# A memory update's tile copied out of PSUM whole, and a new table by slot

## The chip, the cores and the metric

The kernel runs on one core of a Trainium2 chip. The time is device time of that core in microseconds (us). The kernel before took 998.64 us, the median of three runs (998.44 to 998.71). An engine is named as the profile names it: PE is TensorE's matmuls and PEld its weight loads, DVE is VectorE, ACT ScalarE, POOL GpSimd, and SP the engine that issues the DMAs.

## The reference, cut to what matters

Two attention blocks A and B with a compressive memory read the same input x (2048 x 640) and are mixed by a gate per token. Each block has 32 heads of 20 channels and goes over four segments of 512 tokens:

```python
for s in range(N):
    qs, ks, vs = q[:, :, s], k[:, :, s], v[:, :, s]
    logits = jnp.einsum("bhqd,bhkd->bhqk", qs, ks) * scale + mask
    p = _softmax(logits, axis=-1)
    a_dot = jnp.einsum("bhqk,bhkd->bhqd", p, vs)
    pq = phi(qs)
    num = jnp.einsum("bhld,bhde->bhle", pq, M)
    den = jnp.einsum("bhld,bhd->bhl", pq, z)[..., None] + 1e-6
    a_mem = num / den
    o = g * a_mem + (1.0 - g) * a_dot
    outs.append(o)
    pk = phi(ks)
    M = M + jnp.einsum("bhld,bhle->bhde", pk, vs)
    z = z + jnp.einsum("bhld->bhd", pk)
```

phi(t) is t + 1 above zero and exp(t) below; the mask is causal. M (20 x 20 a head) and z (20 a head) are the memory; the last two lines are its update, which the change is about.

## The kernel before, in words

**Tiling.** The 640 channels are five tiles m of 128. A pair of block and segment is a t from 0 to 7 (block t % 2, segment t // 2). For each t there are jobs of TensorE: the projections q and k by tile, v by half, and the output projection o. Each product is split into high and low parts and into the two halves of the array, 64 rows each, so that two matmuls can run side by side. Eight quads of four heads in each t give 64 units i. A unit has scores for the row maxima (`s_unit`, L1288, read by VectorE at L1275), scores transposed for the exponentials (`t_unit`, L1372, read by ScalarE at L1364, masked by POOL at L1365), and the product with v (`pv_unit`, L1392). All of these take one of the eight PSUM banks and give it back when the reading engine is through.

**The memory's update.** M and z of a block lie in five tiles `mbd` of 128 partitions by (heads of the tile) x 21 columns: 7 heads and 147 columns, or 8 and 168 for m = 2. Only where a row's channel belongs to the column's head is the entry wanted. After a `pv_unit`, `updates()` takes up to three tiles whose keys are there and lets TensorE make them in one bank, side by side (L1031). For each tile it goes over four windows of 32 partitions, and each window makes only the two or three heads that touch its rows, 42 or 63 columns. What stands in the tile's other columns of the bank is left from whatever used the bank before. `updated()` then has VectorE copy the four windows out (`take`, L1052), into `mbd` itself in the first segment, and into one of two tiles `mt` in the later ones. POOL sets to zero what is not an own head, by two selections (`keep_own_heads`, L377 and L381), and in the later segments adds the tile to `mbd` (L1057). `mt` is free again after the add; the bank when the copies of all its updates are through. Because the copies fill only the windows, `mbd` and `mt` are set to zero once at the start (L373).

**What sets the order.** Nothing is scheduled by hand on the chip: a planner in the kernel plays the run through with costs for each piece, and emits each engine's instructions in the order in which its play reaches them. `put(engine, cost, emit, then, prio)` queues a piece on ScalarE (A), VectorE (D), POOL (G) or the DMA queue (S); where two engines could do it, the one with less queued work gets it. TensorE's pieces are emitted one by one, each half of the array with its own clock (`op`), and a bank is taken when the play holds it free. The engines run their queues in order, so where a piece is later on the chip than in the play, everything behind it on its engine waits, and so does TensorE when the bank that it takes next is not yet empty. In the play an update costs TensorE 8 x `UPD` = 8 x (63 / 1200 + 0.0027) = 0.4416 us, its copies begin 0.2 us after its own matmuls and cost VectorE 0.44 us, and POOL's part costs 0.8 or 1.34 us. A table `RULES` gives 66 slots, one for each unit and two more, an order of the unit's ten pieces and seven numbers that shift when they are due (span, calm, lag, room, hold, wait, wait2).

Of the kernel before, what the change touches and what calls it, by code (L numbers as in the profile page):

```python
# [19 lines left out]
D = 640  # L20
# [12 lines left out]
LO = [P * m // DH for m in range(KT)]  # L33
# [9 lines left out]
def tile_gated_mix_infini_attn(  # L43
# [17 lines left out]
    nc = tc.nc  # L61
# [26 lines left out]


    RULES = {  # L90
# [66 lines left out]
    }  # L157
    rule = {}
    DONE = {"A": 0.27, "D": 0.26, "G": 0.22, "S": 0.0}
# [13 lines left out]
    def first_of(dur):  # L173
        return dur[0] if isinstance(dur, tuple) else dur

    def start_next(e):
        if busy[e] or not ready[e]:
            return
        if e == "S":
            begin_at = max(dma_free[0] - BACKLOG, lands[-LANES] if len(lands) >= LANES else 0.0)  # L180
            if begin_at > clk[0]:
                if not held[0]:
                    held[0] = True
                    at(begin_at, resume)
                return
        _, _, dur, emit, then = heapq.heappop(ready[e])
        base = first_of(dur)
        if base is not dur:
            dur = dur[1] if busy["G"] else dur[0]
        busy[e] = True  # L190
        emit()

        def end():
            busy[e] = False
            load[e] -= base
            if then and e == "S":
                then()
            elif then:
                at(clk[0] + DONE[e], then)
            start_next(e)  # L200

        at(clk[0] + dur, end)
# [9 lines left out]
    def put(e, dur, emit, then=None, prio=5):  # L212
        heapq.heappush(ready[e], (prio, next(seq), dur, emit, then))
        load[e] += first_of(dur)
        start_next(e)
# [115 lines left out]
    mbds = [[const.tile([P, HI[m] - LO[m] + 1, E1], F32, name=f"mbd{b}_{m}") for m in range(KT)] for b in range(2)]  # L331
# [34 lines left out]
    def ones_tiles():  # L366
        for t in vst:
            h = t[:, :, :H * E1].rearrange("p n (h e) -> p n h e", e=E1)
            nc.gpsimd.memset(h[:, :, :, DH], 1.0)
            nc.gpsimd.memset(h[:, :, H // 2, :12], 1.0)  # L370
            nc.gpsimd.memset(t[:, :, H * E1:], 1.0)
        for t in (*mbds[0], *mbds[1], *mt_store.free):
            nc.gpsimd.memset(t, 0.0)  # L373

    def keep_own_heads(t, m):
        nh, off = HI[m] - LO[m] + 1, P * m - DH * LO[m]
# [113 lines left out]
    for t in range(8):  # L490
        a = 0 if t == 0 else 8 * t - EARLY
# [511 lines left out]
    mt_store = Store([sb.tile([P, 8, E1], F32, tag=f"mt{i}", name=f"mt{i}", bufs=1) for i in range(2)])  # L1003
# [1 line left out]

    upd_due = deque()
    upd_run = set()
    UPD = 63 / 1200.0 + 0.0027

    def windows(m):  # L1010
        for j in range(4):
            f0 = P * m + 32 * j
            a, c = f0 // DH, (f0 + 31) // DH + 1
            yield slice(32 * j, 32 * j + 32), a, c

    def updates():
# [6 lines left out]
        for x in todo:  # L1023
# [5 lines left out]
            for n in range(NB):  # L1029
                for r, a, c in windows(m):  # L1030
# [4 lines left out]
                    )  # L1035
            now[0] += 8 * UPD
            upd_run.add((t, m))
# [3 lines left out]
    def updated(t, m, pkn, v, done):  # L1041
        s = t // 2
        mbd = mbds[t % 2][m]
        nh = HI[m] - LO[m] + 1

        def end():
            upd_done.add((t, m))

        def take(dst):
            for r, a, c in windows(m):  # L1050
                h = slice(a - LO[m], c - LO[m])
                nc.vector.tensor_copy(dst[r, h, :], v[r, h, :])  # L1052

        def got(tmp):
            def add():
                keep_own_heads(tmp[:, :nh, :], m)
                nc.gpsimd.tensor_tensor(out=mbd, in0=mbd, in1=tmp[:, :nh, :], op=ALU.add)  # L1057

            put("D", 0.44, lambda: take(tmp), lambda: (
                done(), put("G", 1.34, add, lambda: (mt_store.give(tmp), end()), prio=2)), prio=3)  # L1060

        big.give(pkn)
        if s == 0:
            put("D", 0.44, lambda: take(mbd), lambda: (
                done(), put("G", 0.8, lambda: keep_own_heads(mbd, m), end, prio=2)), prio=3)
        else:
            mt_store.want(1, got)
# [695 lines left out]

    warm_up()
    put("G", 6.0, small_tiles, prio=0)
    put("G", 2.8, ones_tiles, prio=1)
    big.want((F32,) * 4, lambda *rows: (x_first_rows.extend(rows), x_first.give(*rows[:3])))
    for k in range(KT):
        if k < len(HEAD0):
# [9 lines left out]
    for i in range(66):  # L1779
# [11 lines left out]
        for j in range(10):  # L1791
            fill_to(marks[i] - rule["hold"] + rule["span"] * (j + 1) / 10 * (marks[i + 1] - marks[i]))
            c = todo[0]
            if c == "S" and i + LEAD < 64 and "T" in todo and not S(i + LEAD, 0)() and T(i, 0)():
                c = "T"
# [63 lines left out]
```

## Time and profile before

| | before |
|---|---|
| median of three runs | 998.64 us (998.44 to 998.71) |
| the profiled execution's own time | 997.83 us |
| its span, first to last instruction | 996.1 us |
| granted clock of TensorE | 1.000 |
| copies of line 1052 | 120 |
| groups of updates on TensorE | 12, six of two tiles and six of three |

The profile is of one execution. The span is cut into what each engine did; "busy" on PE is modelled, so the waits of PE and PEld say more than its share. In a row of a group stand line, engine, operation, output and input with shapes, count, then busy us and mean ns of one, then the idle time in front of them and what ended it. In a row of the timeline stand start and length in us, the instruction, its count, and in brackets the idle time before it and who ended it.

### The profile page before, as it was taken

How to read it: one execution, taken by the hardware profiler on the slowest of the kernel's cores; microseconds unless marked ns; L12 is line 12 of the kernel's file. 1: busy time of each engine (PE TensorE's matmuls, PEld its weight loads, DVE VectorE, ACT ScalarE, POOL GpSimd, SP SyncE). 2: the span in 40 equal slices, each digit the busy share in tenths (PEclk: the TensorE clock that was granted, in tenths of full speed). 3: DMA queues.
4: the chain of work that ended last, by engine and by line, in shares of the span. 5: the costliest groups of instructions: out<-in, count | busy, mean ns of one | idle time of the engine just before them, and what ended most of it. 6: DMA issues, size and time to landing. Idle time of an engine off the chain costs nothing.

```text
span 996.1 us, 31535 instructions
## 1 busy us (share of the span) xinstructions
PE 979.4 (98%) x11559; PEld 821.2 (82%) x11559; DVE 814.0 (82%) x2904; ACT 654.4 (66%) x1310; POOL 604.5 (61%) x1052
## 2 busy tenths in 40 slices
PE   9999999999999999999999999999999999999998
PEld 7987888778897888987888877889788987879776
DVE  4796978887798977897879988888788997799874
ACT  5366777676586667685685746776577575675572
POOL 5455656766466765675654676576656664666561
PEclk9999999999999999999999999999999999999999
DMA  7987889898797876976759796789667987887521
GB/s 248 311 281 237 291 234 299 261 279 262 239 307 238 272 214 202 319 241 187 225 173 311 212 283 199 211 270 269 195 214 226 295 279 217 239 251 209 142 90 65
DMA packets 146453, 236.47 MB, mean 237 GB/s; under 512 B 12949, under 2 KB 45882, under 8 KB 145978
## 3 DMA queue, kind: packets, MB, share of 16 engines
q1 hardware_dynamic: 146298, 234.46, 76.4%
q8 instruction: 91, 1.49, 0.6%
q14 instruction: 64, 0.52, 0.2%
HBM read 145.26 MB, written 94.65 MB: 241 GB/s over the span
## 4 chain that ended last, share of the span: by engine, by line
PE 84%; DVE 7%; DMA 4%; issue 2%; POOL 2%; SPq 1%; ACT 1%; DVEq 0%; ACTq 0%; POOLq 0%
PE bank L820 51%; PE bank L1392 13%; PE bank L1288 7%; PE bank L1372 7%; PE bank L973 2%; PE bank L931 2%; DMA row<-dots 1%; DVE mt L1052 1%; DVE bank L1275 1%; DVE mbd L1052 1%; PE bank L1031 1%; DMA row<-rowg 1%; DMA dots<-row 1%; DMA kd<-row 1%; DVE mr L1311 1%
## 5 line engine op out<-in xcount | busy, mean ns | idle before, releaser
L1275 DVE CUSTOM_DVE_ANT_0 bank<-bank,tri 128x384 f32<-128x384 f32 (+3 forms) x1024 | 474.4, 520 | 86.6 <-PE bank L1288 75.0
L820 PE MATMUL bank<-row,wh 64*128 64x512 f32 x2308 | 479.7, 402 | 0.2
L1364 ACT ACTIVATE p<-bank 128x512 f32<-128x512 f32 x550 | 301.5, 605 | 141.5 <-PE bank L1372 113.4
L820 PEld LDWEIGHTS bank<-row,wh 64*128 64x128 f32 x2308 | 308.6, 185 | 16.8 <-PE bank L820 1.8
L1365 POOL TENSOR_SCALAR_AFFINE_SELECT p<-p 128x128 f32<-128x128 f32 (+1 forms) x550 | 203.4, 378 | 188.3 <-ACT p L1364 171.6
L820 PE MATMUL bank<-row,wl 64*128 64x512 f32 x1154 | 292.7, 398 | 0.0
L557 POOL TENSOR_TENSOR wl<-wst,wh 128x640 fp32r<-128x640 f32 x115 | 180.5, 1578 | 61.5 <-ACT wh L559 49.3
L1288 PE MATMUL bank<-kst,qst 60*128 60x384 f32 (+3 forms) x1024 | 174.2, 317 | 6.6 <-DVE mt L1052 2.8
L820 PEld LDWEIGHTS bank<-row,wl 64*128 64x128 f32 x1154 | 172.2, 185 | 7.7 <-issue 1.0
L1372 PE MATMUL bank<-qst,kst 62*128 62x128 f32 (+3 forms) x1024 | 172.8, 319 | 2.3 <-DVE mt L1052 0.9
L820 PE MATMUL bank<-wvh,row 64*128 64x320 f32 (+1 forms) x1280 | 166.0, 312 | 0.6 <-DVE row L770 0.6
L1275 DVE DVE_READ_ACCUMULATOR2_ANT mx<- 128x1 f32 x1024 | 144.4, 141 | 0.2
L1288 PEld LDWEIGHTS bank<-kst,qst 60*128 60x128 f32 x1024 | 128.3, 185 | 18.6 <-DVE mbd L1052 3.9
L820 PEld LDWEIGHTS bank<-wvh,row 64*128 64x128 f32 x1280 | 140.7, 185 | 3.1 <-DVE row L770 0.9
L1392 PE MATMUL bank<-p,vst 128*32 128x384 f32 (+3 forms) x1840 | 141.8, 423 | 0.0
L1372 PEld LDWEIGHTS bank<-qst,kst 62*128 62x128 f32 x1024 | 127.8, 186 | 17.0 <-DVE mx L1275 3.9
L1392 PEld LDWEIGHTS bank<-p,vst 128*32 128x32 f32 x1840 | 57.4, 110 | 82.2 <-issue 58.7
L559 ACT CAST wh<-wst 128x640 fp32r<-128x640 f32 x119 | 86.2, 744 | 34.2 <-PE bank L820 18.8
L820 PE MATMUL bank<-wvl,row 64*128 64x320 f32 (+1 forms) x640 | 99.4, 311 | 0.0
L820 PEld LDWEIGHTS bank<-wvl,row 64*128 64x128 f32 x640 | 80.7, 186 | 0.6 <-issue 0.4
L1311 DVE STREAM_TRANSPOSE mr<-mt 32x32 f32<-32x32 f32 x256 | 51.0, 199 | 26.9 <-POOL mt L1300 24.2
L1423 ACT COPY row<-bank 128x512 f32<-128x512 f32 x58 | 34.4, 594 | 56.4 <-PE bank L1392 51.5
(121 smaller groups left out, 1146.2 us busy)
## 6 DMA issues: line engine op xcount, KB each, us to landing
qst<-qd SPq DMA_DIRECT2D x128, 240.0 KB
kst<-kd SPq DMA_DIRECT2D x128, 240.0 KB
qd<-row SPq DMA_DIRECT2D x40, 512.0 KB
kd<-row SPq DMA_DIRECT2D x40, 512.0 KB
dots<-row SPq DMA_DIRECT2D x56, 256.0 KB
wst<-wmix SPq DMA_DIRECT2D x35, 320.0 KB
row<-dots SPq DMA_DIRECT2D x42, 256.0 KB
qd<-row SPq DMA_DIRECT2D x40, 256.0 KB
```

Source lines behind the costliest of these rows:

```text
L557: put(lo_eng, lo_cost, lambda: lo.tensor_tensor(out=wl, in0=w3, in1=r32(wh), op=ALU.subtract), end, prio=3)
L559: put("A", 0.625, lambda: nc.scalar.copy(wh, w3), low, prio=6)
L820: return nc.tensor.matmul(bank_of, lhsT=w[ROWS[half]], rhs=x_[ROWS[half]], start=start, stop=stop)
L931: return nc.tensor.matmul(pm[:, a - h0:c - h0, :].rearrange("p h e -> p (h e)"), lhsT=r32(pqTs[t, m][ROWS[half], P * n:P * (n + 1)]), rhs= ...
L1275: put("D", w / 960.0 + 0.105, lambda: nc.vector.tensor_tensor_reduce(out=sc[:, off:off + w], in0=sc[:, off:off + w], in1=tri[:, L - w:], s ...
L1288: lane_ops[half].append((mm(w), lambda pair=pair, qb=qb, off=off, w=w, r=r, sc=sc: nc.tensor.matmul(sc[:, off:off + w], lhsT=q[r, pair, P ...
L1311: nc.vector.transpose(r32(mr[:, 32 * j:32 * j + 32]), r32(mt[32 * j:32 * j + 32, :]))
L1364: put("A", 0.483, lambda: nc.scalar.activation(pt, sc, AF.Exp, scale=SCALE), lambda: (bank.give(sc), put("G", 0.15 + 0.105 * len(todo), la ...
L1365: "G", 0.15 + 0.105 * len(todo), lambda: nc.gpsimd.affine_select(out=blocks, in_=blocks, pattern=[[0, len(todo)], [1, P]], base=0, channel ...
L1372: lane_ops[half].append((mm(w), lambda pair=pair, kb=kb, off=off, w=w, r=r, sc=sc: nc.tensor.matmul(sc[:, off:off + w], lhsT=k[r, pair, P ...
L1392: nc.tensor.matmul(po[32 * j:32 * j + 32, P * kb:], lhsT=vst[t % 2][:, kb, h * E1:h * E1 + 32], rhs=pts[i, n, f][0][:, off:off + w], start ...
L1423: either(0.483, lambda: nc.scalar.copy(r32(oT), po), 0.605, lambda: nc.vector.tensor_copy(r32(oT), po), end, 2)
```

## The change

An update's tile leaves PSUM in one copy over all 128 partitions and all its columns, the stale ones among them; POOL's two selections then set everything outside the own heads to zero, as before. So 120 copies become 30. The zeros at the start go, since nothing reads what a copy has not written. Three costs of the planner change: the copies from 0.44 to 0.22 us, an update on TensorE from 0.4416 to 8 x 0.047 = 0.376 us, and POOL's first fills from 2.8 to 1.6 us. The table by slot is another one in all of its 66 rows. TensorE's matmuls are the same in kind and number.

```diff
@@ RULES
-        0: "TSTSTSTSTS 1.01 2.38 0.23 8 0 1.6 1",
-        1: "SSTSTSTSTT 1.01 2.38 0.34 8 1.4 1.6 1",
...
+        0: "TTTSSTSTSS 1.01 2.38 0.3 8 0 1.6 1",
+        1: "TSTSTSTSTS 1.01 2.38 0.22 8 1.6 1.6 1",
...
@@ ones_tiles
-        for t in (*mbds[0], *mbds[1], *mt_store.free):
-            nc.gpsimd.memset(t, 0.0)
@@
-    UPD = 63 / 1200.0 + 0.0027
+    UPD = 0.047
@@ updated
-        def take(dst):
-            for r, a, c in windows(m):
-                h = slice(a - LO[m], c - LO[m])
-                nc.vector.tensor_copy(dst[r, h, :], v[r, h, :])
-
         def got(tmp):
             def add():
                 keep_own_heads(tmp[:, :nh, :], m)
                 nc.gpsimd.tensor_tensor(out=mbd, in0=mbd, in1=tmp[:, :nh, :], op=ALU.add)

-            put("D", 0.44, lambda: take(tmp), lambda: (
+            put("D", 0.22, lambda: nc.vector.tensor_copy(tmp[:, :nh, :], v), lambda: (
                 done(), put("G", 1.34, add, lambda: (mt_store.give(tmp), end()), prio=2)), prio=3)

         big.give(pkn)
         if s == 0:
-            put("D", 0.44, lambda: take(mbd), lambda: (
+            put("D", 0.22, lambda: nc.vector.tensor_copy(mbd, v), lambda: (
                 done(), put("G", 0.8, lambda: keep_own_heads(mbd, m), end, prio=2)), prio=3)
         else:
             mt_store.want(1, got)
@@
-    put("G", 2.8, ones_tiles, prio=1)
+    put("G", 1.6, ones_tiles, prio=1)
```

Three places show how the order moves. The first is VectorE at the first segment's group of three updates of block A (at 92 us in the trace of before); ISA rows at L1275 or L1268 are the row maxima of the scores. Before:

```order
L786 TENSOR_TENSOR row_1497_1526<-bank_141,row_1496_1525 128x512
L1052 COPY mbd_2_72<-bank_141 32x63
L1052 COPY mbd_2_72<-bank_141 32x42 x2
L1052 COPY mbd_2_72<-bank_141 32x63
L1052 COPY mbd_3_73<-bank_141 32x42
L1052 COPY mbd_3_73<-bank_141 32x63
L1052 COPY mbd_3_73<-bank_141 32x42 x2
L1052 COPY mbd_4_74<-bank_141 32x63
L1052 COPY mbd_4_74<-bank_141 32x42
L1052 COPY mbd_4_74<-bank_141 32x63
L1052 COPY mbd_4_74<-bank_141 32x42
L1275 ISA bank_137,mx_1640<-bank_137,tri 128x512
```

After:

```order
L784 TENSOR_TENSOR row_1587_1550<-bank_135,row_1586_1549 128x512
L1057 COPY mbd_2_72<-bank_138 128x168
L1057 COPY mbd_3_73<-bank_138 128x147
L1057 COPY mbd_4_74<-bank_138 128x147
L1268 ISA bank_140,mx_1482<-bank_140,tri 128x256
```

Twelve copies have become three, and they stand again right ahead of row maxima. The second place is TensorE at the same group: the last of its matmuls (L1031, now L1029), and what follows until the bank of the update is written again. Before:

```order
L1031 MATMUL bank_141<-vst_88,row_1095_1197 32x63
L1031 MATMUL bank_141<-vst_88,row_1095_1197 32x42
L1288 MATMUL bank_137<-kst_85,qst_81 128x512
L1288 MATMUL bank_138<-kst_85,qst_81 128x512
L820 MATMUL bank_134<-row_25_197,wl_146 128x512
L820 MATMUL bank_135<-row_72_233,wl_148 128x512
L820 MATMUL bank_134<-row_72_233,wl_146 128x512
L820 MATMUL bank_135<-row_77_236,wl_148 128x512
L820 MATMUL bank_134<-row_77_236,wl_146 128x512
L1288 MATMUL bank_141<-kst_85,qst_81 128x384
```

After:

```order
L1029 MATMUL bank_138<-vst_88,row_1113_1194 32x63
L1029 MATMUL bank_138<-vst_88,row_1113_1194 32x42
L1281 MATMUL bank_140<-kst_85,qst_81 128x256
L1281 MATMUL bank_134<-kst_85,qst_81 128x256
L1281 MATMUL bank_140<-kst_85,qst_81 128x256
L1281 MATMUL bank_134<-kst_85,qst_81 128x256
L818 MATMUL bank_141<-row_13_193,wh_149 128x512
L818 MATMUL bank_139<-row_13_193,wh_147 128x512
L818 MATMUL bank_141<-row_20_195,wh_149 128x512
L1365 MATMUL bank_138<-qst_83,kst_87 128x384
```

Seven matmuls stand between in both; other pieces are drawn ahead, and it is a transposed score, not one for the maxima, that takes the bank. The third place is VectorE at a group of three of block B's second segment, where the copies go to the two `mt` tiles and the third one needs the first one's tile again. Before:

```order
L1311 STREAM_TRANSPOSE mr_161<-mt_7975 32x32 x4
L1052 COPY mt_159<-bank_137 32x63
L1052 COPY mt_159<-bank_137 32x42 x2
L1052 COPY mt_159<-bank_137 32x63
L1052 COPY mt_158<-bank_137 32x42
L1052 COPY mt_158<-bank_137 32x63
L1052 COPY mt_158<-bank_137 32x42 x2
L1052 COPY mt_159<-bank_137 32x63
L1052 COPY mt_159<-bank_137 32x42
L1052 COPY mt_159<-bank_137 32x63
L1052 COPY mt_159<-bank_137 32x42
L1275 ISA bank_140,mx_8091<-bank_140,tri 128x512
```

After:

```order
L1304 STREAM_TRANSPOSE mr_160<-mt_7755 32x32 x4
L1052 COPY mt_159<-bank_138 128x147
L1052 COPY mt_158<-bank_138 128x147
L1052 COPY mt_159<-bank_138 128x168
L1268 ISA bank_141,mx_7733<-bank_141,tri 128x384
```

The three copies stand in a row in both, with row maxima behind them.

128 rows, old and new, of the table RULES are left out of this document.

## The prediction

> **What bounds the kernel now.** I read the page's busy shares first, then who waited for whom, then the timeline around the longest waits of TensorE, then the groups by form.
>
> ```profile
> span 996.1 us, 31535 instructions
> PE 979.4 (98%) x11559; PEld 821.2 (82%) x11559; DVE 814.0 (82%) x2904; ACT 654.4 (66%) x1310; POOL 604.5 (61%) x1052
> PE 84%; DVE 7%; DMA 4%; issue 2%; POOL 2%; SPq 1%; ACT 1%; DVEq 0%; ACTq 0%; POOLq 0%
> ```
>
> TensorE is busy for 979.4 of 996.1 us and holds 84% of the chain that ended last, so its own order sets the time. What another engine can give back is the rest, 16.7 us, plus the time in which only one half of the array works, which no row separates. Who owns the 16.7 us is the next view, the waits of TensorE's matmuls (PE) and weight loads (PEld): us in total, times, longest.
>
> ```profile
> PE bank L1288 <- DVE mt L1052: 2.8, 3, 1.2
> PE bank L1288 <- DVE mbd L1052: 2.8, 3, 1.7
> PE bank L1372 <- DVE mt L1052: 0.9, 2, 0.5
> PE bank L1372 <- DVE mbd L1052: 0.6, 1, 0.6
> PEld bank L1288 <- DVE mbd L1052: 3.9, 3, 2.1
> PEld bank L1288 <- DVE mt L1052: 3.6, 3, 1.7
> PEld bank L1372 <- DVE mt L1052: 1.8, 3, 0.8
> PEld bank L1372 <- DVE mbd L1052: 1.0, 1, 1.0
> ```
>
> All eight name line 1052, the copies that this change replaces. The matmuls waited 2.8 + 2.8 + 0.9 + 0.6 = 7.1 us in nine waits, the weight loads in front of them 3.9 + 3.6 + 1.8 + 1.0 = 10.3 us: copies worth 2% of VectorE's instructions end 7.1 of TensorE's 16.7 idle us. Why they do is seen at the longest of these waits, in the timelines of TensorE and VectorE at 92 us (start, length, idle before it):
>
> ```profile
> 92.40 1.36 PE L1031 MATMUL bank<-vst,row 128*32 128x63 f32 x96
> 93.69 0.50 PE L1288 MATMUL bank<-kst,qst 60*128 60x512 f32 x2
> 94.02 0.85 PE L820 MATMUL bank<-row,wl 64*128 64x512 f32 x5
> 96.56 0.50 PE L1288 MATMUL bank<-kst,qst 60*128 60x384 f32 x4 [1.69 <-DVE mbd L1052]
> ```
> ```profile
> 93.84 2.67 DVE L1052 COPY mbd<-bank 32x63 f32<-32x63 f32 x12 [3.38 <-PE bank L1031]
> 96.54 0.70 DVE L1275 CUSTOM_DVE_ANT_0 bank<-bank,tri 128x512 f32<-128x512 f32 x1
> ```
>
> Three updates run on TensorE from 92.40 to 93.76. VectorE, idle for 3.38 us until their last matmul, then copies twelve pieces in 2.67 us, 222 ns each or 0.89 us an update. TensorE has seven matmuls to do and stands still until 96.56: its next score matmuls write the very bank that the copies empty. The plan in the code gives each update's copies 0.44 us, half of that, and releases the first update's copies before the third update's matmuls. By its constants the last copy ends 3 x 0.4416 + 0.2 + 0.44 = 1.96 us after the updates begin; on the chip 93.84 + 2.67 - 92.40 = 4.11 us, or 2.15 late, of which 1.69 (matmul) to 2.1 (weight load) came through as a wait. So the slack at this place was 0.05 to 0.46 us. A pair of updates has more:
>
> ```profile
> 65.20 0.97 PE L1031 MATMUL bank<-vst,row 128*32 128x42 f32 x64
> 68.05 0.57 PE L1288 MATMUL bank<-kst,qst 60*128 60x512 f32 x2 [0.27 <-DVE mbd L1052]
> ```
> ```profile
> 66.23 1.76 DVE L1052 COPY mbd<-bank 32x42 f32<-32x42 f32 x8 [0.93 <-PE bank L1031]
> ```
>
> Planned 2 x 0.4416 + 0.2 + 0.44 = 1.52, measured 66.23 + 1.76 - 65.20 = 2.79: 1.27 late, and 0.27 of it reached the matmul, which leaves a slack of 1.0 us.
>
> **The copies.** Their cost by form, beside the nearest full-width copy out of PSUM:
>
> ```profile
> L1052 DVE COPY mt<-bank 32x42 f32<-32x42 f32 x48 | 9.5, 197 | 4.6 <-PE bank L1031 2.3 <-issue 1.2
> L1052 DVE COPY mt<-bank 32x63 f32<-32x63 f32 x32 | 7.0, 219 | 3.8 <-PE bank L1031 2.5 <-POOL mbd L1057 0.7
> L1052 DVE COPY mbd<-bank 32x42 f32<-32x42 f32 x24 | 4.8, 198 | 3.5 <-PE bank L1031 3.1
> L1052 DVE COPY mbd<-bank 32x63 f32<-32x63 f32 x16 | 3.5, 219 | 3.6 <-PE bank L1031 3.4
> L1423 DVE COPY row<-bank 128x512 f32<-128x512 f32 x6 | 4.1, 682 | 1.1 <-PE bank L1392 1.1
> ```
>
> 120 copies, 9.5 + 7.0 + 4.8 + 3.5 = 24.8 us. A copy of 128 x 147 or 128 x 168 does not occur before; it lies between these rows. From 42 to 63 columns the price rises by 22 ns, 1.05 ns a column, and from 63 to 512 by 463 ns, 1.03 a column, so 105 columns more give 197 + 110 = 307 ns for 147 and 329 for 168. All 128 partitions cost no more than 32, if the 512 row may be read so: it is on the same line through the points with 32 partitions. Thirty copies: 24 x 0.307 + 6 x 0.329 = 9.3 us, 15.5 less. As the queue sees it an update's copies take 0.31 us in place of 0.89, while the plan now gives 0.22.
>
> What is gained is not these 15.5 us, since most of them lay beside running matmuls, but the waits: **7.1 us** by the matmuls' rows, **10.3** by the weight loads' (an empty array needs its weights before it can start, so the truth is between). I take the middle, 8.7.
>
> **What of the waits stays.** The copies will still wait for the last matmul of their group. With the same start as at 92 us, the last of three copies ends 1.44 + 0.307 + 0.307 + 0.329 = 2.38 us after the updates begin. The plan now says 3 x 0.376 + 0.2 + 0.22 = 1.55: 0.83 late against 2.15, and with 0.05 to 0.46 us of slack a wait of 0.4 to 0.8. A pair ends at 1.03 + 0.61 = 1.64 against 1.17: 0.47 late, inside its slack of 1.0. Both orders have six groups of three and six of two, and only a group whose bank is written again at once can wait, so the remainder lies between 0 and 6 x 0.4 = 2.4; I take the middle, **1.2 back**.
>
> [...]
>
> **The order.** The new table by slot moves nearly every instruction. At the group of three at 92 us (the second place shown with the change) the update's bank was written again after seven matmuls, five of them of 512 columns. It still is after seven, and these are shorter, four of 256 columns: so this place, where the old order waited longest, is the likeliest to keep a rest. On all of TensorE I counted the neighbours in both orders by the half of the array that each names (the printed rows leave it out): matmuls that follow one on the same half rather than the other, transposes and the 84-column ones apart, are 710 before and 784 now, 74 more. Same-half neighbours can't run side by side. The price is nothing where the next weight load hides behind the other half, and at most a whole load where it does not:
>
> ```profile
> L820 PE MATMUL bank<-row,wh 64*128 64x512 f32 x2308 | 479.7, 402 | 0.2
> L820 PEld LDWEIGHTS bank<-row,wh 64*128 64x128 f32 x2308 | 308.6, 185 | 16.8 <-PE bank L820 1.8 <-DVE mx L1275 0.7 <-issue 0.6
> ```
>
> That is 0 to 74 x 0.185 = 13.7 us. The matmuls of this largest group were idle for 0.2 us in 2308, so loads are nearly always hidden, and the price is near the low end. I take 20 ns each, **1.5 us lost**. The set of matmuls is the same.
>
> **Costed at nothing.** The twelve memsets:
>
> ```profile
> 7.60 1.74 POOL L373 MEMSET mbd<- 128x147 f32 x10
> 9.26 0.43 POOL L373 MEMSET mt<- 128x168 f32 x2
> 9.62 0.22 POOL L659 MEMSET row<- 128x128 f32 x1
> ```
>
> They leave POOL's queue 2.0 us earlier at 9.6 us; behind them stands the row for the gate's weights, which TensorE transposes among its first products, and POOL does nothing else until 16 us. The tiles need no zero any more, because each copy fills them whole and the two selections on POOL then overwrite what is not an own head. If something of the start did hang on it, the gain would be up to 2.0 more. VectorE's 15.5 freed us are partly taken up by other work that the plan shares out by load (nine more copies of transposed keys, six more two-step clamps); with TensorE bound that is cover, not path.
>
> **The sum.** -8.7 + 1.2 + 1.5 = -6.0 us. The profiled execution took 997.8 us by its own clock, 1.7 more than its span, and the median of the three shown is 0.8 above it, so 998.6 becomes **992.6 us**. The ends: -10.3 with no rest and no loss gives 988.3, and -7.1 + 2.4 + 3.0 (twice my price for the order) gives 996.9.
>
> **Rivals.**
>
> *The wait moves to POOL.* There are two mt tiles, so the third update of a group waits until POOL has masked and added the first. The third place shown with the change has three such copies in a row, before and now. The maxima behind the third copy, which free score banks, are stuck with it. For it speak
>
> ```profile
> 469.11 0.93 DVE L1052 COPY mt<-bank 32x63 f32<-32x63 f32 x4 [0.73 <-POOL mbd L1057]
> L377 POOL TENSOR_SCALAR_AFFINE_SELECT mt<-mt 128x147 f32<-128x147 f32 (+1 forms) x20 | 7.9, 393 | 11.8 <-DVE mt L1052 11.8
> L381 POOL TENSOR_SCALAR_AFFINE_SELECT mt<-mt 128x147 f32<-128x147 f32 (+1 forms) x20 | 7.4, 370 | 1.4
> L1057 POOL TENSOR_TENSOR mbd<-mbd,mt 128x147 f32<-128x147 f32 (+1 forms) x20 | 10.2, 509 | 1.7
> ```
>
> POOL needs 0.39 + 0.37 + 0.51 = 1.27 us, while the second copy now covers only 0.31: 0.96 us uncovered, in up to four groups, 3.8 us. Against it: the plan knows POOL's time, and in three of the four, other work stands in between. It gives -6.0 + 3.8 = -2.2, 996.4 us.
>
> *Another holder.* The bank stays occupied for a cause that the copies only masked (VectorE's maxima, ScalarE's exponentials), and the same waits appear under another name: 998.6. Against it, the matmul at 96.56 starts 0.05 us after the copies end.
>
> *More than the rows say.* The page's chain gives about 1% of the span to each of the two kinds of copies:
>
> ```profile
> PE bank L820 51%; PE bank L1392 13%; PE bank L1288 7%; PE bank L1372 7%; PE bank L973 2%; PE bank L931 2%; DMA row<-dots 1%; DVE mt L1052 1%; DVE bank L1275 1%; DVE mbd L1052 1%; PE bank L1031 1%; DMA row<-rowg 1%; DMA dots<-row 1%; DMA kd<-row 1%; DVE mr L1311 1%
> ```
>
> Counted as path, 2% is 20 us. With 0.31 / 0.89 of each copy left, 13 would go, and less 1.5 for the order the time is 987. Against it, TensorE worked during most of it.
>
> *Slower: the new order packs the halves worse.* If each of the 74 added neighbours pays its whole weight load, 13.7 us are lost against 8.7 - 1.2 = 7.5 won: 6.2 slower, 1004.8 us. It decides from 7.5 / 74 = 101 ns each. Against it stands the 0.2 us of idle matmuls above.
>
> **Chances.** Forecast 0.60, POOL 0.12, another holder 0.09, more 0.09, slower 0.10. No change means within 0.2% here, 996.6 to 1000.6, about what a measurement of this kernel tells apart. The forecast is faster but for 0.03, POOL's case lies on the border and is split in half, so faster is 0.57 + 0.06 + 0.09 = 0.72, the same 0.03 + 0.06 + 0.09 = 0.18, slower 0.10. The likeliest case's own range is 988.3 to 996.9. Widened to hold the unknown neighbours and half of the other cases, the range is 987.5 to 999.0.
>
> **What would show it.** Right: thirty copies of 128 x 147 and 128 x 168 at about 307 and 329 ns; TensorE's waits for the update copies down from 7.1 to 1 or 2 us, the rest at groups of three; TensorE busy about as long as before, within 3 us. Wrong: copies near 0.5 us; waits of the same sum that name maxima or POOL; a longer busy time of TensorE without waits, which is the order; a third copy that waits over 1 us for POOL.

## The result, and the profile after

The changed kernel takes **988.78 us** (median of four runs, 987.82 to 989.17) against 998.67 us of the kernel before on the same chip: 9.9 us less, a ratio of 0.990 with an interval of 0.988 to 0.9915. On another chip it was 987.99 against 997.72, 0.991 (0.989 to 0.9925). The forecast was 992.6, so the direction was right and the gain larger than its sum, 9.9 us in place of 6.0. The profiled execution took 989.17 us, 1.8 more than its span.

The page of the changed kernel, its span, its busy times and its chain by engine:

```profile
span 987.4 us, 31435 instructions
PE 977.6 (99%) x11559; PEld 825.5 (84%) x11559; DVE 798.8 (81%) x2825; ACT 646.9 (66%) x1297; POOL 604.0 (61%) x1042
PE 93%; DMA 2%; DVE 2%; POOL 1%; ACT 1%; issue 1%; SPq 0%; POOLq 0%; ACTq 0%
```

TensorE's idle time fell from 16.7 to 987.4 - 977.6 = 9.8 us, and its share of the chain rose from 84% to 93%. The waits of its matmuls, all of them, and of its weight loads as far as they name the update's copies (lines 1052 and 1057 now):

```profile
PE bank L356 <- DVE qst L360: 1.5, 1, 1.5
PE bank L1281 <- DMA kst<-kd: 1.1, 1, 1.1
PE bank L818 <- ACT p L1357: 0.9, 1, 0.9
PE bank L1365 <- DVE mx L1268: 0.7, 2, 0.4
PE bank L1365 <- ACT row L987: 0.6, 1, 0.6
PE bank L868 <- ACT wh L557: 0.2, 1, 0.2
```
```profile
PEld bank L1365 <- DVE mt L1052: 1.1, 3, 0.5
PEld bank L1365 <- DVE mbd L1057: 0.6, 2, 0.4
PEld bank L818 <- DVE mt L1052: 0.2, 1, 0.2
```

No matmul waits for an update's copy any more (7.1 us before), and the weight loads wait 1.9 us (10.3 before). What is left has other owners, each once or twice. The copies by form, and the group of three that was shown at 92 us, on TensorE and on VectorE:

```profile
L1052 DVE COPY mt<-bank 128x147 f32<-128x147 f32 x16 | 4.3, 303 | 7.4 <-PE bank L1029 7.3
L1057 DVE COPY mbd<-bank 128x147 f32<-128x147 f32 x8 | 2.1, 302 | 0.1
L1052 DVE COPY mt<-bank 128x168 f32<-128x168 f32 x4 | 1.3, 330 | 2.6 <-POOL mbd L1050 1.5 <-PE bank L1029 1.1
L1057 DVE COPY mbd<-bank 128x168 f32<-128x168 f32 x2 | 0.7, 326 | 2.3 <-PE bank L1029 2.3
```
```profile
91.86 1.36 PE L1029 MATMUL bank<-vst,row 128*32 128x63 f32 x96
93.15 0.50 PE L1281 MATMUL bank<-kst,qst 60*128 60x256 f32 x4
93.50 0.63 PE L818 MATMUL bank<-row,wh 64*128 64x512 f32 x3
94.13 0.51 PE L1365 MATMUL bank<-qst,kst 62*128 62x384 f32 x4
```
```profile
93.31 0.77 DVE L1057 COPY mbd<-bank 128x168 f32<-128x168 f32 x3 [2.35 <-PE bank L1029]
94.00 0.42 DVE L1268 CUSTOM_DVE_ANT_0 bank<-bank,tri 128x256 f32<-128x256 f32 x1
```

Three copies, of about 0.30 us each for 147 columns and 0.33 for 168, take 0.77 us together: the second and third start 0.25 and 0.22 us after the one ahead, 84 and 83 ns before it has ended. Twelve took 2.67. The bank is free at 94.08, and TensorE writes it at 94.13 with no gap behind the three matmuls in front.

### The profile page after: what moved, and what is told of

The parts are those of the page before. It is cut to its first block, busy times and chain, and to the rows that moved or that the text cites. A ratio compares the mean times of both kernels' runs of the same rounds, so it can differ in the third digit from the quotient of the medians.

```text
span 987.4 us, 31435 instructions
## 1 busy us (share of the span) xinstructions
PE 977.6 (99%) x11559; PEld 825.5 (84%) x11559; DVE 798.8 (81%) x2825; ACT 646.9 (66%) x1297; POOL 604.0 (61%) x1042
## 4 chain that ended last, share of the span: by engine, by line
PE 93%; DMA 2%; DVE 2%; POOL 1%; ACT 1%; issue 1%; SPq 0%; POOLq 0%; ACTq 0%
PE bank L818 56%; PE bank L1385 14%; PE bank L1365 8%; PE bank L1281 8%; PE bank L929 3%; PE bank L971 3%; PE bank L1029 1%; DMA kst<-kd 1%; PE bank L868 1%; DMA row<-rowg 1%; DMA row<-dots 1%; PE bank L1210 0%; DMA wst<-in_a_wk_dram 0%; POOL p L1358 0%; DVE bank L1268 0%
## 5 line engine op out<-in xcount | busy, mean ns | idle before, releaser
L1268 DVE CUSTOM_DVE_ANT_0 bank<-bank,tri 128x256 f32<-128x256 f32 (+3 forms) x1024 | 474.5, 520 | 90.3 <-PE bank L1281 81.8
L818 PE MATMUL bank<-row,wh 64*128 64x512 f32 x2308 | 487.4, 401 | 0.9 <-ACT p L1357 0.9
L818 PEld LDWEIGHTS bank<-row,wh 64*128 64x128 f32 x2308 | 315.5, 185 | 15.5 <-ACT p L1357 1.2
L1358 POOL TENSOR_SCALAR_AFFINE_SELECT p<-p 128x256 f32<-128x256 f32 (+1 forms) x546 | 200.0, 376 | 174.5 <-ACT p L1357 161.0
L818 PE MATMUL bank<-wvh,row 64*128 64x320 f32 (+1 forms) x1280 | 177.8, 312 | 0.1
L818 PEld LDWEIGHTS bank<-wvh,row 64*128 64x128 f32 x1280 | 150.4, 185 | 2.0 <-ACT p L1357 0.4
L1268 DVE DVE_READ_ACCUMULATOR2_ANT mx<- 128x1 f32 x1024 | 145.2, 142 | 0.0
L1385 PE MATMUL bank<-p,vst 128*32 128x256 f32 (+3 forms) x1816 | 139.9, 425 | 0.0
L818 PE MATMUL bank<-wvl,row 64*128 64x320 f32 (+1 forms) x640 | 105.7, 311 | 0.0
L557 ACT CAST wh<-wst 128x640 fp32r<-128x640 f32 x119 | 87.3, 745 | 20.2 <-PE bank L818 12.8
L818 PEld LDWEIGHTS bank<-wvl,row 64*128 64x128 f32 x640 | 85.2, 186 | 0.7 <-issue 0.2
L530 POOL TENSOR_TENSOR wvl<-wst,wvh 128x640 fp32r<-128x640 f32 (+1 forms) x48 | 60.2, 1260 | 17.6 <-ACT wvh L674 9.2
```

What stands on the lines that cost most here:

```text
L530: put("G", 0.77 * n, lambda: nc.gpsimd.tensor_tensor(out=wl[:, a:b, :VN], in0=w3, in1=r32(wh[:, a:b, :VN]), op=ALU.subtract), end, prio=4)
L557: put("A", 0.625, lambda: nc.scalar.copy(wh, w3), low, prio=6)
L818: return nc.tensor.matmul(bank_of, lhsT=w[ROWS[half]], rhs=x_[ROWS[half]], start=start, stop=stop)
L1268: put("D", w / 960.0 + 0.105, lambda: nc.vector.tensor_tensor_reduce(out=sc[:, off:off + w], in0=sc[:, off:off + w], in1=tri[:, L - w:], s ...
L1358: "G", 0.15 + 0.105 * len(todo), lambda: nc.gpsimd.affine_select(out=blocks, in_=blocks, pattern=[[0, len(todo)], [1, P]], base=0, channel ...
L1385: nc.tensor.matmul(po[32 * j:32 * j + 32, P * kb:], lhsT=vst[t % 2][:, kb, h * E1:h * E1 + 32], rhs=pts[i, n, f][0][:, off:off + w], start ...
```

## The experiments

Each experiment keeps the whole computation. Where the order on TensorE is said to be that of another kernel, it is the same matmul for matmul.

### The two parts apart

The copies and the order can be crossed, since the plan decides the order from its own costs and not from what is emitted. The old order with the new copy:

```diff
 (kernel before: old table, old costs)
-            put("D", 0.44, lambda: take(tmp), ...
+            put("D", 0.44, lambda: nc.vector.tensor_copy(tmp[:, :nh, :], v), ...
-            put("D", 0.44, lambda: take(mbd), ...
+            put("D", 0.44, lambda: nc.vector.tensor_copy(mbd, v), ...
-        for t in (*mbds[0], *mbds[1], *mt_store.free):
-            nc.gpsimd.memset(t, 0.0)
```

> The order of the kernel before on TensorE, matmul for matmul, with its old table and old plan costs, but each update's tile leaves PSUM in one copy (no zeros at the start). If the waits are the cause, the 7.1 (matmuls) to 10.3 us (weight loads) of waits for the copies fall to under 1 us, since 0.31 us is less than the 0.44 us that this plan allows, and the time is 988.5 to 991.5 us. If the order is the cause, it stays at 997 to 999 us. If the table costs 1.5 us by its worse pairing of halves, as predicted, this kernel is 1 to 2 us faster than it would be with the new table and the same waits.

Measured: 984.25 us, ratio to before 0.986 (0.985 to 0.988), 4 us below the bottom of what I expected. The copy alone wins 14.2 us, more than the whole change. The page's span and busy times, and the place at 92 us on TensorE and on VectorE:

```profile
span 981.6 us, 31429 instructions
PE 973.0 (99%) x11559; PEld 822.1 (84%) x11559; DVE 793.5 (81%) x2814; ACT 653.4 (67%) x1310; POOL 600.2 (61%) x1040
```
```profile
90.97 1.36 PE L1029 MATMUL bank<-vst,row 128*32 128x63 f32 x96
92.25 0.50 PE L1281 MATMUL bank<-kst,qst 60*128 60x512 f32 x2
92.59 0.86 PE L818 MATMUL bank<-row,wl 64*128 64x512 f32 x5
93.23 0.51 PE L1281 MATMUL bank<-kst,qst 60*128 60x384 f32 x4
```
```profile
92.41 0.77 DVE L1057 COPY mbd<-bank 128x168 f32<-128x168 f32 x3 [3.39 <-PE bank L1029]
```

From the first score matmul to the one that takes the update's bank are 93.23 - 92.25 = 0.98 us; in the kernel before it was 96.56 - 93.69 = 2.87. Because both kernels issue the same matmuls in the same order, their start times can be subtracted one by one. I did so over the two traces: of the 14.5 us between the first and the last matmul's start, about 13 are gained within 9 us of the twelve groups of updates (2.0 at this place, 0.1 to 1.8 at the others); 0.7 lie in the first 17 us, before any update, and the rest at 540 us. In the page's terms, of the 14.5 us by which the span fell, 8.1 are idle time of TensorE (16.7 to 8.6) and 6.4 are its busy time (979.4 to 973.0), although the matmuls and their order are the same.

The new order with the old copies:

```diff
 (changed kernel: new table, new costs)
+        def take(dst):
+            for r, a, c in windows(m):
+                h = slice(a - LO[m], c - LO[m])
+                nc.vector.tensor_copy(dst[r, h, :], v[r, h, :])
-            put("D", 0.22, lambda: nc.vector.tensor_copy(tmp[:, :nh, :], v), ...
+            put("D", 0.22, lambda: take(tmp), ...
 (the same for mbd; the zeros at the start are back)
```

> The changed kernel's instruction order on TensorE, matmul for matmul, but each update's tile leaves PSUM in four copies of 32 partitions again (and the zeros at the start are back). If the waits for the copies are what the change won, they come back larger than in the kernel before, since this plan allows 0.22 us where the copies need 0.89: TensorE's matmuls wait 9 to 14 us for line 'take', and the time is 998 to 1003 us. If the new order carries the gain, the time stays within 2 us of the changed kernel's 988.8 us.

Measured: 1005.64 us, ratio 1.008 (1.006 to 1.009), 16.9 us above the changed kernel and 2.6 above the top of what I expected. TensorE's waits for the copies are back, 9.3 us of the 9 to 14 expected:

```profile
PE bank L1372 <- DVE mt L1052: 4.3, 4, 1.4
PE bank L1372 <- DVE mbd L1052: 3.2, 3, 1.9
PE bank L820 <- DVE mt L1052: 1.0, 1, 1.0
PE bank L1288 <- DVE mt L1052: 0.8, 1, 0.8
```

So the copies carry the gain in either order, 14.2 us in the old and 16.9 in the new, and the matmuls' rows of waits, 7.1 us before and 9.3 here, state about half of it. Part of the 16.9 may be the clock's: in this trace TensorE's granted clock is 0.50 for 3.4 us behind the group at 92 us (shown in the last section), which by my estimate, half of that time, can cost up to 1.7 us, and the mean granted clock of the four runs was 0.996 to 0.998, against 0.999 to 1.000 in the changed kernel's. The new order costs time with either copy: 988.8 against 984.3, 1005.6 against 998.4.

### The order's price on one chip

> The changed kernel again, beside the old order with one copy on the same chip, since the two were timed on different ones (988.8 and 984.3 us). If the new order costs what it seemed, this is 4 to 5 us slower than the other; if it was the chip, within 1 us.

> The old order with one copy again, beside the changed kernel: 983.5 to 985 us, 4 to 5 us faster than it if the new order costs them.

Measured: 987.99 and 983.80 us, ratios to the same runs of before 0.991 (0.989 to 0.9925) and 0.986 (0.985 to 0.988). The new order costs 4.2 us, within the 4 to 5 that were expected. **The old order with one copy is faster than both kernels of this case.**

### How long a copy may take

```diff
-            put("D", 0.44, lambda: nc.vector.tensor_copy(mbd, v), ...
+            put("D", 0.44, lambda: (nc.vector.tensor_copy(mbd, v), nc.vector.tensor_copy(mbd, v)), ...
 (the same for tmp; in the old order, and with 0.22 in the new one)
```

> The order of the kernel before on TensorE, each whole copy made twice: an update holds VectorE for about 0.61 us, where this plan allows 0.44. Between one copy (984.3 us) and four (998.4 us). If every us by which the copies end late is paid in full, (0.61 - 0.31) / (0.89 - 0.31) of 14.1 us: 991.6 us. If there is slack first, as I read at the pairs, 986 to 989 us. In the changed kernel's order the same second copy cost 6.3 us; if the tighter plan there leaves less slack, this one costs less than 6.3.

> The changed kernel with each whole copy made twice, one after the other, same order on TensorE: an update holds VectorE for about 0.61 us in place of 0.31. Theory of waits: the response is not proportional, there is slack first. The last of three copies ends 1.44 + 6 x 0.31 = 3.3 us after the updates begin, against 1.55 in the plan; pairs 1.03 + 1.24 = 2.3 against 1.17. With 0.05 to 1.0 us of slack, 2 to 6 us of waits and 991 to 995 us. If VectorE's time at these places does not matter: within 1 us of the changed kernel.

Measured: 990.46 us, ratio 0.992 (0.991 to 0.994), in the old order, 6.2 above one copy and between the two forecasts (986 to 989 with slack first, 991.6 without); 995.13 us, ratio 0.997 (0.996 to 0.998), in the new, 6.3 above it and at the upper edge of its 991 to 995. The second copy costs the same in both, so the tighter plan does not show here. The group of three at 92 us on VectorE, in the old order:

```profile
93.22 1.82 DVE L1057 COPY mbd<-bank 128x168 f32<-128x168 f32 x6 [3.39 <-PE bank L1029]
```

And a third length, by four copies that all begin at partition 0:

```diff
+        def take(dst):
+            for a in range(0, nh, 2):
+                h = slice(a, min(a + 2, nh))
+                nc.vector.tensor_copy(dst[:, h, :], v[:, h, :])
-            put("D", 0.44, lambda: nc.vector.tensor_copy(mbd, v), ...
+            put("D", 0.44, lambda: take(mbd), ...
 (the same for tmp; old order)
```

> The order of the kernel before on TensorE; an update's tile in four copies again, but each over all 128 partitions and two heads (42 columns, the last 21 where there are seven), no zeros at the start. It keeps the number of copies and takes away that each begins at another partition. If the four copies cost 0.89 us because each instruction waits for the one ahead when the starting partition changes, these follow each other at about their length less 80 ns, 0.11 to 0.14 us: 0.5 us an update, and the time is 986 to 990 us. If the number alone counts, they follow at 0.2 us, 0.8 us an update, and the time is 995 to 998 us.

Measured: 986.82 us, ratio 0.9885 (0.987 to 0.990), as the first of the two cases had it. The group of three on VectorE:

```profile
92.94 1.35 DVE L1050 COPY mbd<-bank 128x42 f32<-128x42 f32 x12 [3.38 <-PE bank L1029]
94.21 0.69 DVE L1273 CUSTOM_DVE_ANT_0 bank<-bank,tri 128x512 f32<-128x512 f32 x1
```

Twelve copies of 42 columns (two of them of 21) take 1.35 us where twelve of 42 and 63 columns in four windows took 2.67. So it was not their number: these twelve, which all begin at partition 0, follow each other at about 0.11 us, and the twelve with a new starting partition each time at 0.22. Ordered by what the group of three at 92 us costs VectorE, with the time of the whole kernel in us:

| copies | the group at 92 us | old order | new order |
|---|---|---|---|
| one whole | 0.77 us | 984.3 | 988.8 |
| four by columns | 1.35 us | 986.8 | |
| one whole, twice | 1.82 us | 990.5 | 995.1 |
| four windows | 2.67 us | 998.4 | 1005.6 |

The old plan allows 3 x 0.44 = 1.32 us. Up to there 0.58 us more cost 2.6 us of the whole; beyond, 0.47 us cost 3.6 and 0.85 us cost 7.9, so 8 to 9 us for one. If each of the six groups of three paid in full and each pair two thirds of it, it would be 10. That fits the slack I spoke of, with most of the groups paying behind it. In the new order 1.05 us cost 6.3 and the next 0.85 cost 10.5, part of which is the halved clock named above.

### The zeros at the start

> The kernel of the old order with one copy, and the twelve memsets on POOL at the start kept: 2.0 us more on POOL at 8 us. If, as I costed it, nothing at the start hangs on them: 984.3 us, the same within 0.3 us. If the first products do (in the trace the old kernel is 0.7 us later than this one in the first 17 us): 985 us; at most 986.3.

The loop of the twelve memsets put back into the old order with one copy: 984.32 us, against 984.25 without, ratio to before 0.986 (0.984 to 0.988). Nothing hangs on them that these times could tell.

### The plan and its table

> All of the change but the table by slot: one copy, the new costs of the plan, the old 66 rows. The plan now comes out another way: same-half neighbours on TensorE (transposes and the 84-column matmuls apart) are 960, against 784 with the new table and 710 before. At the 20 ns each that I priced, 176 more than the changed kernel cost 3.5 us: 992 us. At a whole weight load of 185 ns they cost 33 us: 1021 us. If the table does not matter, 989 us.

The changed kernel with the 66 old rows: 1051.39 us, ratio 1.055 (1.051 to 1.058), 62.6 above the changed kernel. None of the three cases comes near it.

> The kernel before with nothing changed but the table by slot: four copies, old costs, the new 66 rows. If a table fits only the plan that it was chosen for, this is as far off as the old table under the new plan (1051 us): same-half neighbours 992, and 1030 to 1070 us. If the new table is worse or better by itself, 995 to 1005 us.

The kernel before with the 66 new rows: 1066.7 us in a single run, 68 above the kernel before and inside the first case's range.

> The changed kernel with one number changed: the plan's cost of a copy 0.31 us, what the copy takes on the chip, in place of 0.22. The waits for copies can only get fewer. But the order comes out anew under a table that was not chosen for it: same-half neighbours on TensorE 973, against 784 in the changed kernel and 960 in the one with the old table (1051 us). If the pairing of halves decides, 1040 to 1060 us; if a truer plan is a better one, under 988.8 us.

```diff
-            put("D", 0.22, lambda: nc.vector.tensor_copy(tmp[:, :nh, :], v), ...
+            put("D", 0.31, lambda: nc.vector.tensor_copy(tmp[:, :nh, :], v), ...
 (the same for mbd)
```

1021.6 us in a single run: neither the 988.8 of "a truer plan is a better one" nor the 1040 of my price. With the other's table either plan is 60 to 70 us slower than with its own. The neighbours that I counted do not tell how much, so I counted something else over the traces' start times: stretches of more than 0.25 us in which one half of the array starts nothing although its last matmul is through (8 ns and 0.438 ns a column, as they follow each other on one half in the trace of before: 120 ns for 256 columns, 233 for 512; the other half's run beside them, at 94.02 us 6 to 8 ns later). Half of their sum is in the fourth column, since each such stretch idles half of the array; at half clock they read somewhat too long, and a count like this is good to a few us. The last column leaves out the end of the run.

| kernel | time, us | same-half neighbours | long idle halves, us | TensorE at half clock, us |
|---|---|---|---|---|
| old order, one copy | 984.3 | 710 | 19 | 0 |
| changed | 988.8 | 784 | 24 | 0 |
| before | 998.7 | 710 | 32 | 0 |
| true cost in the plan | 1021.6 | 973 | 50 | 10 |
| new plan, old table | 1051.4 | 960 | 73 | 48 |
| old plan, new table | 1066.7 | 992 | 91 | 31 |

The long stretches rise with the time; the neighbours don't (960 and 973 are 30 us apart, 710 and 710 14). Between the first two kernels the stretches differ by 5 us and the times by 4.2 to 4.5; between the first and the kernel before, the same order with other copies, by 13 us and 14.4. That they cause it was not tried: none of the kernels changes only them.

## Why the prediction was right or wrong

**The price of the copies: right.** 303 and 302 ns against 307, 330 and 326 against 329. In these copies 128 partitions cost no more than the line through the rows with 32 said. Two readings beside it were off and carry nothing: the 120 copies are 4% of VectorE's 2904 instructions and not 2%, and all seven matmuls between the update and the next use of its bank have 512 columns in the kernel before, not five.

**The term of the waits, -8.7 us: mis-sized; the copies were worth -14.2.** This is the step that failed. I took the middle between the rows of matmuls (7.1) and of weight loads (10.3) that name line 1052. The reason I gave for it, that an empty array needs its weights first, agrees with the trace at the longest wait: the weight load at 96.56 us begins 1 ns ahead of its matmul of 384 columns, and the next matmul on that half follows 0.28 us later, where the spacing of a running stream would give 0.18. The mechanism and the places were right: about 13 us are gained around the twelve groups. But a late copy reaches TensorE also through what stands behind it on VectorE, and that wait carries the later instruction's name. Weight loads of the kernel before at 328 to 336 us, 190.5 to 195.5 us and 595.5 to 600 us, each right after a group of three or two:

```profile
PEld bank L820 <- DVE mx L1275: 0.5, 1, 0.5
PEld bank L1372 <- DVE row L770: 0.5, 1, 0.5
...
PEld bank L1372 <- DVE mx L1275: 0.6, 1, 0.6
...
PEld bank L1372 <- DVE mx L1275: 0.9, 2, 0.6
```

These 2.5 us and the 10.3 make 12.8. The whole run says the same: with one copy in the old order, the weight loads' waits that name the copies add up to 0.4 us in place of 10.3, and those that name the maxima (mx) to 6.4 in place of 9.4. I read only the rows that name the copies; even the weight loads' sum was a lower bound and not an upper one. I had also named the time in which only one half of the array works, and then put it at nothing, since no row separates it. It stands inside TensorE's busy time: 6.4 of the 14.5 us that one copy wins in the old order are busy time of the same matmuls, and the idle halves fall from 32 to 19 us in my count. And a matmul's row counts only what is left when the modelled end of the matmul ahead has passed: at 92 us it says 1.69, where 2.87 - 0.98 = 1.89 us were lost.

**What of the waits stays, +1.2: small, as said, if over-estimated.** No matmul waits for a copy, and the weight loads' waits are 1.9 us in pieces of at most 0.5. The copies did start after the last matmul of their group, as I assumed, but the three take 0.77 us and not 0.94: they follow each other at 0.23 us with a length of 0.30 to 0.33. The four-window copies do not overlap so: at 92 us in the trace of before each starts 13 to 32 ns after the one ahead has ended. The two ways of making four copies, 0.11 and 0.22 us apart, show the difference by themselves.

**The order, +1.5: the sign was right, the price was not, 4.2 us.** 74 more same-half neighbours at 20 ns were the term; 4.2 us would be 57 ns each, but the kernels with tables that do not fit show that the count is no price at all. The idle matmuls of the largest group, 0.2 us, on which I set the low end, say nothing about a half that stands idle beside a busy one: TensorE counts as busy then. TensorE's busy time, 977.6 us against 979.4, looked like my sign of being right (within 3 us), but it is the sum of two changes: 973.0 with the new copies in the old order, and 4.6 more with the new order (973.7 and 976.8 in the second pair of traces). The sign that I had named for the order, a longer busy time without waits, was there and was hidden by the copies' gain. What in the new order costs the 4.2 us stays open; the idle halves are the likeliest, and no run changes only them.

**The sum.** -8.7 + 1.2 + 1.5 = -6.0 stands against -14.2 + 4.2 = -10.0 from the experiments and -9.9 measured. For the copies I had -7.5, with what stays of the waits, 6.7 too little; for the order 2.7 too little; and the two partly cancelled. That the time lay inside both ranges, 0.5 us above the lower end of the likeliest case's own, is in part luck: the copies' gain alone, at 984.3 us, lies outside both.

**Costed at nothing.** Right for the zeros (984.32 against 984.25). VectorE's busy time fell from 814.0 to 798.8 us, 15.2 against the 15.5 of the copies.

**The rivals.** The wait for POOL is there on VectorE, once, and longer than the 0.96 us that I worked out; it is one of the signs that I had named for being wrong:

```profile
456.16 0.53 DVE L1052 COPY mt<-bank 128x147 f32<-128x147 f32 x2 [1.46 <-PE bank L1029]
457.99 0.33 DVE L1052 COPY mt<-bank 128x168 f32<-128x168 f32 x1 [1.30 <-POOL mbd L1050]
```

1.30 us for the third copy of a group, and 0.2 at one other group; but the copies' part before it is 1.28 us shorter than it was (0.53 us, against 1.81 at the group of 466 us before), so the third still ends earlier after its group than before, and TensorE's matmuls have no wait there. "Another holder" did not come: the matmuls' waits name maxima for 0.7 us in all. "More than the rows say" was nearest in size: it took 13 us for the copies, where 14.2 were measured and the forecast had 7.5, and its 987 us is 1.8 from the measured time, the forecast's 992.6 is 3.8. It was given 0.09, and against it I had only that TensorE worked during most of the copies; with one half idle it counts as working. The slower rival named the part that does cost, the order, and missed that the gain it had to beat was twice what I took.

## What to carry to other kernels

Where one engine runs a fixed order, add to the waits that name a late instruction those that name what is queued behind it, within a few us of the place; the rows of the instruction alone were 7.1 to 10.3 us for a loss of 14. Where two halves of an array work side by side, a busy array can still lose time in one of them: here the long idle halves came to 32 us with the four copies and to 19 with one, for the same matmuls in the same order. When a change brings a faster operation and a new schedule together, time the operation in the old schedule: here it was 4 us better than the change. And a table that was tuned against a plan belongs to that plan: one cost corrected by 0.09 us, with the table kept, made the kernel 33 us slower in the one run of it.

## What the runs showed of the hardware

That TensorE's granted clock falls to 0.5 in some of these traces I had not expected. The kernel with the new plan and the old table has its clock at 0.5 in four stretches, 47.8 us in all; before the longest, two matmul starts are 2.8 us apart. In all four of its runs the mean granted clock was 0.972 to 0.980. By my estimate from the 0.5, at most half of these 47.8 us, 24, belong to the clock and not to the waits. By windows (length; busy times of PE, PEld, DVE, ACT and POOL with counts; clock; DMA share; GB/s):

```profile
250.00:289.00 39.00, 39.00 (x429) 33.92 (x426) 29.95 (x115) 25.95 (x54) 17.34 (x33) 1.00 0.87 280
289.00:292.80 3.80, 1.29 (x14) 0.72 (x13) 2.51 (x9) 3.52 (x11) 3.80 (x7) 1.00 0.97 364
292.80:316.70 23.90, 19.41 (x134) 15.91 (x135) 18.30 (x34) 7.30 (x13) 15.36 (x14) 0.50 0.43 135
```

The kernel with the true cost in the plan has it with far less idle time, from 936.7 us on:

```profile
930.00:936.70 6.70, 6.21 (x70) 5.18 (x66) 6.63 (x21) 5.88 (x13) 6.03 (x10) 1.00 0.02 5
936.70:943.50 6.80, 6.54 (x32) 5.11 (x31) 5.72 (x28) 1.11 (x3) 1.79 (x5) 0.50 0.69 162
```

In the 6.7 us before, TensorE was idle for 0.49 us in all, and the longest space between two starts was 0.72, where the first case had 2.8. Here the clock fell while the array was busy for 93% of the time. What sets it in such a stretch, these runs do not tell.

Two of the runs with slower copies have such a stretch as well, the new order with four copies (first row) and with the copy twice (second row):

```profile
97.40:100.70 3.30, 3.30 (x22) 2.96 (x22) 2.29 (x12) 1.47 (x4) 0.99 (x3) 0.50 0.22 82
199.20:202.50 3.30, 3.30 (x17) 2.17 (x18) 3.10 (x9) 1.62 (x4) 2.69 (x5) 0.50 1.07 227
```

The largest spaces between two matmul starts in the 9 us before were 2.3 and 1.4 us, and the first of them is the wait for the copies at 92 us. The traces of the kernel before, of the changed kernel and of the old order with one copy have no such stretch before the last matmul. The first and the last of these are 14.5 us apart, so what the copies gain in the old order is not the clock's.
